# First attention of a fused attention and expert kernel: split q and k for the last three pairs of heads

## The chip, the cores and the metric

The kernel runs on one core of one Trainium2 chip. The metric is the device time of the program in microseconds (us); lower is better. Before the change the median of three runs is 1208.19 us (1207.63 to 1209.15).

## The reference

Four batches of eight heads, 768 positions and 64 columns a head go through softmax attention with a mask and a bias by distance. The result, as rows of 512, goes through four experts whose outputs are added with weights from `domain_probs`.

```python
scores = scale * np.matmul(q, k.transpose(0, 1, 3, 2))        # (4, 8, 768, 768)
is_global = pos[None, :] < int(n_global)                      # 8
is_local = (rel >= 0) & (rel < int(n_local))                  # 96
scores = scores + bias[None, :, :, :]
scores = np.where(keep, scores, -1000000000.0)
a = np.exp(scores - np.max(scores, axis=-1, keepdims=True))
a = a / (np.sum(a, axis=-1, keepdims=True) + 1e-09)
x = (a @ v) as rows of 3072 x 512
for e in range(4):
    h = np.maximum(x @ w1[e], 0.0)
    out += p[:, e:e + 1] * (h @ w2[e])
```

A row of 128 queries needs only the keys of its own tile of 128, the last 96 of the tile before, and the 8 global keys.

## The kernel before, in words

**Attention.** Heads go in pairs, two times 64 columns on 128 partitions. A pair has six tiles of 128 queries. For each tile and head the scores are one block of 256 keys (128 in a first tile): 32 columns of global keys and 96 of the tile before, then 128 of the tile itself.

`attention` (L480) is a generator; each call of its inner `flow` (L486) is one step of a pipeline over tiles. In the step of tile n, `scores` (L386) does the matmuls of tile n into the PSUM tile `ps`, `softmax` (L407) works on the two tiles before, `turn` (L448) transposes the normalised weights `pb` of tile n-3 through PSUM (`pt`) to `pT`, and after every third tile `weigh` (L460) multiplies `pT` by v (`px`) and copies the result to `x`. In `softmax`, VectorE (DVE) adds scores and bias and takes the row's extreme (`nmax`, the operation that the profile calls CUSTOM_DVE_ANT_0), ScalarE (ACT) does exp with the sum to `zsum`, DVE adds 1e-9 to `zsum` (L434), takes the reciprocal (L431) and multiplies `pb` by it (L442).

**Two ways of preparing q and k.** The first batch is computed before any expert work (`early`), the three others are woven into the expert stage.

- Early, `prepare_early` (L358): TensorE (PE) transposes three tiles of q or k of a pair into `pt`. For q, ACT writes the first head's half (L366) and DVE the second's (L370; ACT for the first half of the first pair, L368) into a tile `early_q`, whose other partitions are zeros from `po.memset` (L552, L553, two such tiles); for k, ACT copies both heads at once (L375) and GpSimd (POOL) repeats the global keys (L377). Scores are one full f32 matmul a head (L394).
- Later batches, `prepare_q` (L327) and `prepare_k` (L340): every value is split into a rounded part (F32R) and the rest. For q, ACT writes the rounded part to `st_q` (L331), DVE the rest (L332), and four DMAs on SP's queue place the two heads on the partitions where they are needed, into `qd` (L338). For k, ACT casts each head's half (L351), DVE writes the rests on the other half of the partitions (L354), and DVE repeats the global keys (L356). Scores are two F32R matmuls a head, always 256 keys wide (L398).

**What sets the order.** While `Ordered.on` is true every instruction keeps its program order on its engine; this holds for the whole first attention and the start of the expert stage. Pairs go in the order 0, 2, 1, 3. `prepare_all` (L526) is a generator that prepares one half of q or k at each `next`, and `AHEAD` (L211) says after which tiles the next half comes. In before the order of halves is q, k, k, q for pairs 2 to 4 of that order. In each engine's queue a half stands behind its step's softmax, turn and weigh: on DVE ahead of the next tile's addition of the bias, on ACT behind the two exps, the copy of `pT` and, where there is one, the copy of `x`. SP's queue holds all loads of q, k, v (`start`, L507), the DMAs of shifted v windows (`vg`, L382) and the loads of weights (`raw`, L677, L712), in program order. Chores (L825 to L832) put the splitting of the first experts' weights and of `x` between the steps of the last two pairs.

**Pools** (L824): `st` has one buffer, `qd` one, `kd` two, and there are four `pt` and three `ps` buffers in PSUM.

Of the kernel before, what the change touches and what calls it, by code (L numbers as in the profile page):

```python
# [185 lines left out]
def attn_moe_kernel(ctx: ExitStack, tc, q, k, v, n_global, n_local, domain_probs, w1, w2, out):  # L186
# [88 lines left out]
    class Pools:  # L275


        def __init__(self, stack, name, st, kd, qd, nat, natv, pb, ps, pt, px, early):
            self.early = early

            def sbuf(part, bufs):
                return stack.enter_context(tc.tile_pool(name=f"{name}_{part}", bufs=bufs))

            def psum(part, bufs):
                return stack.enter_context(tc.tile_pool(name=f"{name}_{part}", bufs=bufs, space=PSUM))

            self.st, self.natv = sbuf("st", st), sbuf("natv", natv)
            self.kd, self.qd, self.nat, self.vg = sbuf("kd", kd), sbuf("qd", qd), sbuf("nat", nat), sbuf("vg", kd)
            self.pb, self.pT, self.small = sbuf("pb", pb), sbuf("pT", 4), sbuf("small", pb)
            self.ps, self.pt = psum("ps", ps), psum("pt", pt)  # L290

            self.px, self.pxname = (psum("px", px), "px") if px else (self.pt, "pt")
# [47 lines left out]
    def prepare_k(A, nat, hf, got):  # L340


        tp = transpose_half(A, nat, hf)
        tpv = tp[:, :HALF].rearrange("p (t c) -> p t c", c=P)
        if hf == 0:
            got["k"] = A.kd.tile([P, 2, NQT, PL], F32R, name="kd")
        kd = got["k"]
        pl = slice(hf * TPH, (hf + 1) * TPH)
        for j in range(2):
            own = slice(j * D, (j + 1) * D)  # L350
            ac.copy(kd[own, j, pl, :P], tpv[own])  # L351
        for j in range(2):
            own, oth = slice(j * D, (j + 1) * D), slice((1 - j) * D, (2 - j) * D)
            ve.tensor_tensor(kd[oth, j, pl, :P], tpv[own], f32(kd[own, j, pl, :P]), op=ALU.subtract)  # L354
        if hf == 0:
            ve.tensor_copy(kd[:, :, :, P:], f32(kd[:, :, 0:1, :NGLOB]).to_broadcast([P, 2, NQT, NGLOB]))  # L356

    def prepare_early(A, nat, hf, name, got, zq, first=False):  # L358


        tp = transpose_half(A, nat, hf)
        tpv = tp[:, :HALF].rearrange("p (t c) -> p t c", c=P)
        pl = slice(hf * TPH, (hf + 1) * TPH)
        if name == "q":
            got["q"] = zq
            ac.activation(zq[:D, 0, pl, :], tpv[:D], AF.Copy, scale=-SCALE)  # L366
            if first:
                ac.activation(zq[D:, 1, pl, :], tpv[D:], AF.Copy, scale=-SCALE)  # L368
            else:
                ve.tensor_scalar_mul(zq[D:, 1, pl, :], tpv[D:], -SCALE)  # L370
            return
        if hf == 0:
            got["k"] = A.kd.tile([P, NQT, PL], F32, name="early_k")
        dst = got["k"]
        ac.copy(dst[:, pl, :P], tpv)  # L375
        if hf == 0:
            po.tensor_copy(dst[:, :, P:], dst[:, 0:1, :NGLOB].to_broadcast([P, NQT, NGLOB]))  # L377
# [5 lines left out]
        po.tensor_copy(vg[NPREV:], vt[:NGLOB, :, 0:1, :].to_broadcast([NGLOB, 2, NQT, D]))  # L383
        return vg

    def scores(A, t, got, early):  # L386

        ps = A.ps.tile([P, 2, 2 * P], F32, name="ps")
        c0 = max(t - 1, 0) * PL + (0 if t == 0 else NGLOB)
        n = P if t == 0 else 2 * P  # L390
        for j in range(2):
            if early:
                win = got["k"].rearrange("p t c -> p (t c)")[:, c0 : c0 + n]
                te.matmul(ps[:, j, :n], got["q"][:, j, t, :], win, start=True, stop=True)  # L394
                continue
            win = got["k"][:, j].rearrange("p t c -> p (t c)")[:, c0 : c0 + 2 * P]
            for part in range(2):
                te.matmul(  # L398
                    ps[:, j, : 2 * P],
                    got[("q", t // TPH)][:, j, part, t % TPH * P : (t % TPH + 1) * P],  # L400
                    win,
                    start=(part == 0),
                    stop=(part == 1),
                )
        return ps

    def softmax(A, new, old):  # L407


        if old:  # L410
            pb, zsum = old["pb"], old["zsum"]
        if new:
            t, pr, ps = new["t"], new["pr"], new["ps"]
            cols = slice(0, P) if t == 0 else slice(0, 2 * P)
            bcol = slice(2 * P, 3 * P) if t == 0 else slice(0, 2 * P)
            new["pcol"] = pcol = slice(P, 2 * P) if t == 0 else slice(0, 2 * P)
            nmax = A.small.tile([P, 2], F32, name="nmax")
            new["zsum"] = A.small.tile([P, 2], F32, name="zsum")
            new["pb"] = A.pb.tile([P, 2, 2 * P], F32, name="pb")
        for j in range(2):  # L420
            if new:
                e = new["pb"][:, j, pcol]
                ve.tensor_tensor_reduce(
                    e, ps[:, j, cols], nbias[:, 2 * pr + j, bcol], 1.0, 3.0e38, ALU.add, ALU.min, nmax[:, j : j + 1]
                )
                ac.activation(
                    e, e, AF.Exp, bias=nmax[:, j : j + 1], scale=-1.0, accum_out=new["zsum"][:, j : j + 1]
                )
            if old:
                if j == 1:  # L430
                    ve.reciprocal(zsum, zsum)  # L431
                elif A.early:
                    old["spare"] = A.small.tile([P, 2], F32, name="spare")
                    ve.tensor_scalar_add(zsum, zsum, 1e-9)  # L434
                else:
                    ac.activation(zsum, zsum, AF.Copy, bias=1e-9)
        if old:
            for j in range(2):
                p = pb[:, j, old["pcol"]]
                if A.early:  # L440

                    ve.tensor_scalar(  # L442
                        p, p, zsum[:, j : j + 1], None, op0=ALU.mult, op1=ALU.add, accum_out=old["spare"][:, j : j + 1]
                    )
                else:
                    ac.activation(p, p, AF.Copy, scale=zsum[:, j : j + 1])
# [33 lines left out]
    def attention(b, A, early=False):  # L480
# [5 lines left out]
        def flow(new=None):  # L486

            one, two, three, four = tiles
            if new:
                new["ps"] = scores(A, new["t"], gots[new["pr"]], early)  # L490
            if four:
                turned.append(four)
            ready = len(turned) == TPH
            if ready and not early:
                weigh(A, turned, x)
            if three and not early:
                turn(A, three)
            softmax(A, one, two)
            if three and early:
                turn(A, three)  # L500
            if ready and early:
                weigh(A, turned, x)
            if ready:
                turned.clear()
            tiles[:] = [new, one, two, three]
# [20 lines left out]
        def prepare_all(pr):  # L526

            nat, got = nats[pr], gots[pr]
            got["v"] = nat
            prepare_early(A, nat["q"], 0, "q", got, zqs[PAIRS.index(pr) % 2], first=pr == 0)  # L530
            if pr:
                yield 1
            prepare_early(A, nat["k"], 0, "k", got, zqs[PAIRS.index(pr) % 2])
            yield 1
            nat["vg"] = windows(A, nat["v"])
            prepare_early(A, nat["k"], 1, "k", got, zqs[PAIRS.index(pr) % 2])
            yield 1
            prepare_early(A, nat["q"], 1, "q", got, zqs[PAIRS.index(pr) % 2])
            yield 1

        nats, gots = {}, [{} for _ in range(NPAIR)]
        if early:
# [4 lines left out]
            for h in halves:  # L547
                next(h)
            nats[0]["v"] = next(load(A, v, b, 0, "v"))
            zqs = [A.qd.tile([P, 2, NQT, P], F32, name=f"early_q{n}") for n in range(2)]  # L550
            for zq in zqs:
                po.memset(zq[D:, 0], 0.0)  # L552
                po.memset(zq[:D, 1], 0.0)  # L553
            todo = [prepare_all(pr) for pr in PAIRS]
            next(bias)
            next(todo[0])
# [264 lines left out]
    bp = main.enter_context(tc.tile_pool(name="bp", bufs=1))  # L821
    Ordered.on = True
    with ExitStack() as start_stack:
        A = Pools(start_stack, "start", st=1, kd=2, qd=1, nat=2, natv=3, pb=4, ps=3, pt=4, px=1, early=True)  # L824
        for n, _ in enumerate(attention(0, A, early=True)):  # L825
            if n == 9:
                chores += [load_w1(0, lead=2), load_w2(0, lead=3)]
            if n == 18:
                chores.append(load_w1(1, lead=2, hold=3))
            if n == 2 * NQT + 5:  # L830
                chores.append(blocks(0, (0,), po))
            work_chores()  # L832
        mix = mixture()
        next(mix)
# [85 lines left out]
```

## Time and profile before

| what | value |
|---|---|
| median of three runs | 1208.19 us |
| time of the profiled execution | 1207.05 us |
| its span | 1205.2 us |
| PE busy | 1173.4 us (97%) |
| DVE busy | 830.0 us (69%) |
| ACT busy | 494.8 us (41%) |
| POOL busy | 213.8 us (18%) |
| first attention | from 0 to about 72 us of the span |

The profile is one execution. Its times count from the start of the span; the profiled execution's own time is 1.85 us longer than the span. A row of the time line has the start, the duration, the engine, the line, the operation, what it writes and reads, the shape and, in brackets, how long the engine sat idle before it and what ended this. Nearly every instruction carries L42, the line of the helper that records them, so rows are told apart by the names of tiles. A duration is not the distance to the next start: engines overlap an operation's end with the next one's beginning, so distances between starts are used where a rate matters.

### The profile page before, as it was taken

The page shows a single profiled execution, that of the slowest core. Times are in us where ns is not written, and L with a number is a line of the kernel's source. Part 1 is how long each engine was busy: PE and PEld are TensorE (multiplying, and loading weights), DVE is VectorE, ACT ScalarE, POOL GpSimd, SP SyncE. Part 2 cuts the span into 40 slices and gives each one's busy share as a digit, 9 for nine tenths or more (in the row PEclk, how much of TensorE's full clock was granted, in tenths as well). Part 3 has the DMA queues.
Part 4 walks back from the last instruction along what each step waited for, and adds up shares of the span by engine and source line. Part 5 has one row for each costly group of instructions (what it writes and reads, how often), then busy time and mean ns, then how long its engine had stood idle before and what let it go on. Part 6 is the DMA issues. An engine that isn't in the chain of part 4 may idle for free.

```text
span 1205.2 us, 18090 instructions
## 1 busy us (share of the span) xinstructions
PE 1173.4 (97%) x6624; PEld 1050.4 (87%) x6624; DVE 830.0 (69%) x1841; ACT 494.8 (41%) x1269; POOL 213.8 (18%) x226
## 2 busy tenths in 40 slices
PE   6888999999999999999999999999999999999997
PEld 5677889899889989899898989899898999999996
DVE  6886566666678676676668767576676766666665
ACT  5865656555542444444442444444443211111110
POOL 5546645646450000000002000000000100000000
PEclk9999999999999999999999999999999999999999
DMA  6456786876977656575746757675663655555532
GB/s 164 122 187 213 247 309 224 305 263 243 339 244 251 217 197 210 201 234 171 230 174 201 257 184 221 204 222 169 212 212 133 244 193 193 185 178 183 188 131 90
DMA packets 122704, 251.39 MB, mean 209 GB/s; under 512 B 83184, under 2 KB 91376, under 8 KB 106224
## 3 DMA queue, kind: packets, MB, share of 16 engines
q1 hardware_dynamic: 118864, 243.87, 60.9%
q10 hardware_dynamic: 3744, 6.30, 1.4%
q8 instruction: 54, 0.88, 0.3%
q14 instruction: 42, 0.34, 0.1%
HBM read 174.11 MB, written 52.43 MB: 188 GB/s over the span
## 4 chain that ended last, share of the span: by engine, by line
PE 87%; DVE 3%; DMA 3%; ACT 3%; POOL 2%; issue 2%; SPq 0%; ACTq 0%; POOLq 0%; DVEq 0%
PE pm L42 77%; PE pt L42 6%; PE ps L42 3%; DMA raw<-in_moe_w_dram 2%; DVE pb L42 1%; POOL sums L42 1%; ACT pb L42 1%; POOL w2s L42 1%; DMA qd<-st_q 1%; SPq L42 0%; DVE x L42 0%; DVE zsum L42 0%; DMA raw_ng<-in_n_global_dram 0%; ACT pT L42 0%; ACT w1s L42 0%
## 5 line engine op out<-in xcount | busy, mean ns | idle before, releaser
L42 PE MATMUL pm<-w2s,h 128*128 128x512 f32 x2304 | 551.8, 393 | 4.5 <-DVE h L42 4.5
L42 PEld LDWEIGHTS pm<-w2s,h 128*128 128x128 f32 x2304 | 426.0, 188 | 92.8 <-DVE h L42 6.9
L42 DVE SCALAR_TENSOR_TENSOR acc<-pm,prob,acc 128x512 f32<-128x512 f32 x360 | 268.1, 748 | 148.5 <-PE pm L42 146.3
L42 PE MATMUL pm<-xT,w1s 128*128 128x384 f32 x1536 | 296.5, 338 | 0.2 <-ACT xT L42 0.2
L42 PEld LDWEIGHTS pm<-xT,w1s 128*128 128x128 f32 x1536 | 267.7, 189 | 2.3 <-issue 1.4
L42 PE MATMUL pm<-xB,w1s 128*128 128x384 f32 x1152 | 226.7, 338 | 1.6 <-DVE xB L42 1.3
L42 PEld LDWEIGHTS pm<-xB,w1s 128*128 128x128 f32 x1152 | 201.2, 188 | 6.8 <-DVE xB L42 1.6
L42 ACT ACTIVATE h<-pm 128x384 fp32r<-128x384 f32 x256 | 124.7, 491 | 178.3 <-DVE pm L42 174.8
L42 DVE SCALAR_TENSOR_TENSOR h<-pm,h 128x384 fp32r<-128x384 f32 x256 | 140.7, 552 | 13.6 <-ACT h L42 10.0
L42 ACT ACTIVATE pb<-pb,nmax 128x256 f32<-128x256 f32 (+1 forms) x192 | 93.1, 486 | 102.1 <-DVE nmax L42 97.9
L42 ACT COPY p<-pm 128x384 f32<-128x384 f32 x64 | 30.6, 479 | 190.6 <-PE pm L42 181.7
L42 POOL COPY vg<-v 32x768 f32<-32x768 f32 x16 | 13.2, 823 | 497.6 <-DMA v<-in_v_dram 378.9
L42 DVE TENSOR_TENSOR u<-pm,p 128x384 f32<-128x384 f32 x64 | 35.6, 556 | 73.9 <-PE pm L42 54.3
L42 DVE CUSTOM_DVE_ANT_0 pb<-ps,nbias 128x256 f32<-128x256 f32 (+1 forms) x192 | 71.4, 395 | 8.4 <-PE pt L42 4.7
L42 ACT COPY pT<-pt 128x512 f32<-128x512 f32 (+1 forms) x96 | 52.4, 546 | 56.3 <-PE pt L42 56.0
L42 DVE TENSOR_TENSOR pm<-pm,vv 128x384 f32<-128x384 f32 x128 | 71.6, 560 | 1.6 <-PE pm L42 1.4
L42 ACT ACTIVATE pb<-pb,zsum 128x256 f32<-128x256 f32 (+1 forms) x144 | 63.2, 484 | 18.1 <-DVE zsum L42 18.1
L42 PE MATMUL pt<-ident,pb 128*128 128x128 f32 x352 | 57.5, 277 | 9.1 <-DVE pb L42 5.1
L42 PEld LDWEIGHTS pt<-ident,pb 128*128 128x128 f32 x352 | 42.7, 141 | 19.3 <-ACT pb L42 10.0
L42 DVE TENSOR_TENSOR vv<-pm,u 128x384 f32<-128x384 f32 x64 | 35.7, 557 | 27.7 <-PE pm L42 27.1
L42 DVE TENSOR_TENSOR u<-pm,u 128x384 f32<-128x384 f32 x64 | 35.6, 557 | 25.0 <-PE pm L42 24.3
L42 POOL TENSOR_TENSOR w2s<-raw,w2s 128x512 fp32r<-128x512 f32 x32 | 41.1, 1301 | 57.4 <-ACT w2s L42 50.6
(89 smaller groups left out, 904.4 us busy)
## 6 DMA issues: line engine op xcount, KB each, us to landing
w1s<-kept SPq DMA_DIRECT2D x48, 1792.0 KB, 7.3
w2s<-kept SPq DMA_DIRECT2D x48, 1024.0 KB, 4.9
kept<-w1s SPq DMA_DIRECT2D x16, 1792.0 KB, 9.4
qd<-st_q SPq DMA_DIRECT2D x96, 192.0 KB, 4.7
raw<-in_moe_w_dram SPq DMA_DIRECT2D x32, 512.0 KB, 5.8
kept<-w2s SPq DMA_DIRECT2D x16, 1024.0 KB, 7.1
v<-in_v_dram SPq DMA_DIRECT2D x16, 384.0 KB, 4.0
out_dram<-acc ACTq DMA_DIRECT2D x24, 256.0 KB, 3.3
```

Source lines behind the costliest of these rows:

```text
L42: ins = fn(*args, **kwargs)
```

## The change

In the first attention only the first pair keeps the early form. The three others use `prepare_q` and `prepare_k` with their split parts, DMAs and doubled F32R matmuls; their halves come in the order q, k, q, k, and the shifted windows of v come ahead of the last of them. The early pair's q is now one tile by head, written by ACT in both halves, and only one such tile has its zeros set. The repeat of the global keys in `prepare_k` goes to POOL in the early attention. The addition of 1e-9 writes a third, unused column of `spare` as a sum. `qd` has three buffers.

```diff
-    def prepare_early(A, nat, hf, name, got, zq, first=False):
+    def prepare_early(A, nat, hf, name, got, zq):
...
-            ac.activation(zq[:D, 0, pl, :], tpv[:D], AF.Copy, scale=-SCALE)
-            if first:
-                ac.activation(zq[D:, 1, pl, :], tpv[D:], AF.Copy, scale=-SCALE)
-            else:
-                ve.tensor_scalar_mul(zq[D:, 1, pl, :], tpv[D:], -SCALE)
+            ac.activation(zq[0][:D, pl, :], tpv[:D], AF.Copy, scale=-SCALE)
+            ac.activation(zq[1][D:, pl, :], tpv[D:], AF.Copy, scale=-SCALE)
...
-            ve.tensor_copy(kd[:, :, :, P:], f32(kd[:, :, 0:1, :NGLOB]).to_broadcast([P, 2, NQT, NGLOB]))
+            eng = po if A.early else ve
+            eng.tensor_copy(kd[:, :, :, P:], f32(kd[:, :, 0:1, :NGLOB]).to_broadcast([P, 2, NQT, NGLOB]))
...
-            if early:
+            if early and pr == 0:
...
-                    old["spare"] = A.small.tile([P, 2], F32, name="spare")
-                    ve.tensor_scalar_add(zsum, zsum, 1e-9)
+                    old["spare"] = spare = A.small.tile([P, 3], F32, name="spare")
+                    ve.tensor_scalar(zsum, zsum, 1e-9, None, op0=ALU.add, op1=ALU.add, accum_out=spare[:, 2:3])
...
             if pr:
+                prepare_q(A, nat["q"], 0, got)
                 yield 1
+                prepare_k(A, nat["k"], 0, got)
+                yield 1
+                prepare_q(A, nat["q"], 1, got)
+                yield 1
+                nat["vg"] = windows(A, nat["v"])
+                prepare_k(A, nat["k"], 1, got)
+                yield 1
+                return
...
-            zqs = [A.qd.tile([P, 2, NQT, P], F32, name=f"early_q{n}") for n in range(2)]
-            for zq in zqs:
-                po.memset(zq[D:, 0], 0.0)
-                po.memset(zq[:D, 1], 0.0)
+            zq = f32(A.qd.tile([P, 2, 2, HALF], F32R, name="qd")).rearrange("p j n (t c) -> p j (n t) c", c=P)
+            zq = [zq[:, j] for j in range(2)]
+            po.memset(zq[0][D:], 0.0)
+            po.memset(zq[1][:D], 0.0)
```

How this moves instructions is best seen on DVE in the fifth and sixth tile of the first pair. Before, behind the scaling of `pb` (`pb,spare<-pb,zsum`) the next tile's addition of the bias (`ISA pb,nmax<-ps,nbias`) follows at once, since both steps prepare halves of k on ACT alone:

```order
L42 TENSOR_SCALAR early_q_165<-pt 64x384
L42 ISA pb,nmax<-ps,nbias 128x256
L42 ISA nmax 128x1
L42 TENSOR_SCALAR zsum<-zsum 128x2
L42 ISA pb,nmax<-ps,nbias 128x256
L42 ISA nmax 128x1
L42 RECIPROCAL zsum<-zsum 128x2
L42 TENSOR_SCALAR pb,spare<-pb,zsum 128x256 x2
L42 ISA pb,nmax<-ps,nbias 128x256
```

In the changed kernel two subtractions into `kd` stand at that place:

```order
L42 SCALAR_TENSOR_TENSOR st_q<-pt,st_q 128x384
L42 ISA pb,nmax<-ps,nbias 128x256
L42 ISA nmax 128x1
L42 TENSOR_SCALAR zsum,spare<-zsum 128x2
L42 ISA pb,nmax<-ps,nbias 128x256
L42 ISA nmax 128x1
L42 RECIPROCAL zsum<-zsum 128x2
L42 TENSOR_SCALAR pb,spare<-pb,zsum 128x256 x2
L42 TENSOR_TENSOR kd<-pt,kd 64x3x128 x2
L42 ISA pb,nmax<-ps,nbias 128x256
```

The half of q has kept its place, with another operation; the half of k, which had none on DVE, now has two instructions ahead of the next tile.

The second place is SP's queue from the load of the second next pair's v on. Before:

```order
L42 DMA v<-in_v_dram 128x12x64
L42 DMA vg<-v 96x768
L42 DMA q<-in_q_dram 128x6x64 x2
L42 DMA k<-in_k_dram 128x6x64 x2
L890 TENSOR_LOAD flag
L890 ISA x2
L42 DMA v<-in_v_dram 128x12x64
```

In the changed kernel:

```order
L42 DMA v<-in_v_dram 128x12x64
L42 DMA qd<-st_q 64x768 x4
L899 TENSOR_LOAD flag
L899 ISA x2
L42 DMA qd<-st_q 64x768 x4
L42 DMA vg<-v 96x768
L42 DMA qd<-st_q 64x768 x4
L42 DMA q<-in_q_dram 128x6x64 x2
L42 DMA k<-in_k_dram 128x6x64 x2
L42 DMA v<-in_v_dram 128x12x64
L42 DMA qd<-st_q 64x768 x4
```

Three halves of q, four DMAs each, now stand ahead of the last pair's loads of q and k, and a fourth half comes behind its load of v.

More of the change, by code (lines that the diff above doesn't have):

```diff
@@ L287, in __init__ @@
             self.st, self.natv = sbuf("st", st), sbuf("natv", natv)
+            self.one = sbuf("one", 1) if early else None
             self.kd, self.qd, self.nat, self.vg = sbuf("kd", kd), sbuf("qd", qd), sbuf("nat", nat), sbuf("vg", kd)
@@ L365, in prepare_early @@
             got["q"] = zq
-            ac.activation(zq[:D, 0, pl, :], tpv[:D], AF.Copy, scale=-SCALE)
-            if first:
-                ac.activation(zq[D:, 1, pl, :], tpv[D:], AF.Copy, scale=-SCALE)
-            else:
-                ve.tensor_scalar_mul(zq[D:, 1, pl, :], tpv[D:], -SCALE)
+            ac.activation(zq[0][:D, pl, :], tpv[:D], AF.Copy, scale=-SCALE)
+            ac.activation(zq[1][D:, pl, :], tpv[D:], AF.Copy, scale=-SCALE)
             return
         if hf == 0:
-            got["k"] = A.kd.tile([P, NQT, PL], F32, name="early_k")
+            got["k"] = A.one.tile([P, NQT, PL], F32, name="early_k")
         dst = got["k"]
@@ L384, in windows, with scores @@
         return vg
-    def scores(A, t, got, early):
+    def scores(A, t, pr, got, early):
         ps = A.ps.tile([P, 2, 2 * P], F32, name="ps")
@@ L391, in scores @@
         for j in range(2):
-            if early:
+            if early and pr == 0:
                 win = got["k"].rearrange("p t c -> p (t c)")[:, c0 : c0 + n]
-                te.matmul(ps[:, j, :n], got["q"][:, j, t, :], win, start=True, stop=True)
+                te.matmul(ps[:, j, :n], got["q"][j][:, t, :], win, start=True, stop=True)
                 continue
@@ L489, in flow @@
             if new:
-                new["ps"] = scores(A, new["t"], gots[new["pr"]], early)
+                new["ps"] = scores(A, new["t"], new["pr"], gots[new["pr"]], early)
             if four:
@@ L529, in prepare_all @@
             got["v"] = nat
-            prepare_early(A, nat["q"], 0, "q", got, zqs[PAIRS.index(pr) % 2], first=pr == 0)
             if pr:
+                prepare_q(A, nat["q"], 0, got)
                 yield 1
-            prepare_early(A, nat["k"], 0, "k", got, zqs[PAIRS.index(pr) % 2])
+                prepare_k(A, nat["k"], 0, got)
[6 more added lines that the diff above has]
+                return
+            prepare_early(A, nat["q"], 0, "q", got, zq)
+            prepare_early(A, nat["k"], 0, "k", got, zq)
             yield 1
             nat["vg"] = windows(A, nat["v"])
-            prepare_early(A, nat["k"], 1, "k", got, zqs[PAIRS.index(pr) % 2])
+            prepare_early(A, nat["k"], 1, "k", got, zq)
             yield 1
-            prepare_early(A, nat["q"], 1, "q", got, zqs[PAIRS.index(pr) % 2])
+            prepare_early(A, nat["q"], 1, "q", got, zq)
             yield 1
@@ L823, in attn_moe_kernel @@
     with ExitStack() as start_stack:
-        A = Pools(start_stack, "start", st=1, kd=2, qd=1, nat=2, natv=3, pb=4, ps=3, pt=4, px=1, early=True)
+        A = Pools(start_stack, "start", st=1, kd=2, qd=3, nat=2, natv=3, pb=4, ps=3, pt=4, px=1, early=True)
         for n, _ in enumerate(attention(0, A, early=True)):
```

## The prediction

> **What bounds the kernel now.** The page's chain of what ended last gives 87% of the span to TensorE, but almost all of that is the expert stage. The change touches only the first attention, so I read the stage table for it, then the chain of its first 78 us, then the time line of VectorE (DVE) and ScalarE (ACT) one step at a time.
>
> First the stage table (columns: stretch in us, its length, busy time of PE, PEld, DVE, ACT, POOL, then granted clock, DMA share, GB/s). The first row runs from the step of the third tile to the step behind the last preparation, the second from there to the first expert matmul. Behind it stands the chain by line of 0 to 78 us.
>
> ```profile
> 15.91:48.85 32.94, 29.48 (x232) 23.63 (x232) 26.94 (x137) 27.21 (x86) 15.39 (x19) 1.00 0.52 143
> 48.85:72.28 23.43, 19.05 (x154) 14.26 (x152) 20.20 (x100) 20.94 (x62) 15.81 (x17) 0.93 0.26 56
> by line: DVE pb L42 17.7%; ACT pb L42 10.1%; DMA raw<-in_moe_w_dram 8.8%; PE ps L42 4.8%; DVE zsum L42 4.6%; DMA raw_ng<-in_n_global_dram 4.6%; issue 4.5%; ACT pT L42 4.5%; DVE x L42 4.2%; PE px L42 3.8%; DVE early_q L42 3.6%; PE pt L42 3.4
> DVE early_q L42 <- ACT early_q L42: 7.3, 7, 1.9
> PE pt L42 <- DVE pb L42: 5.1, 8, 1.2
> ```
>
> PE, DVE and ACT are all 82 to 89% busy, so busy shares decide nothing. The chain does: it goes through softmax work of DVE and ACT, and the score matmuls (ps) carry 4.8%. The waits (who waited for whom: total us, times, longest) say the same: PE waits for the softmax of the tile before, and DVE waits 7.3 us for ACT's half of q.
>
> A step is one `flow` call. I count it from the first scores-plus-bias operation (CUSTOM, pb<-ps) of one tile to that of the next. DVE's time line, in pieces:
>
> ```profile
> 18.72 0.42 DVE L42 CUSTOM_DVE_ANT_0 pb<-ps,nbias 128x256 f32<-128x256 f32 x1
> 20.48 0.42 DVE L42 CUSTOM_DVE_ANT_0 pb<-ps,nbias 128x256 f32<-128x256 f32 x1
> ...
> 25.86 0.29 DVE L42 CUSTOM_DVE_ANT_0 pb<-ps,nbias 128x128 f32<-128x128 f32 x1
> 27.36 0.08 DVE L42 DVE_READ_ACCUMULATOR pb<-pb,zsum 128x1 f32 x1
> 28.02 0.56 DVE L42 TENSOR_SCALAR early_q<-pt 64x384 f32<-64x384 f32 x1 [0.58 <-ACT early_q L42]
> 28.59 0.42 DVE L42 CUSTOM_DVE_ANT_0 pb<-ps,nbias 128x256 f32<-128x256 f32 x1
> ...
> 48.85 0.42 DVE L42 CUSTOM_DVE_ANT_0 pb<-ps,nbias 128x256 f32<-128x256 f32 x1
> ```
>
> A step in which half a k is prepared (18.72 to 20.48) takes 1.76 us, DVE's own work, because DVE has nothing to do for k. A step with half a q (25.86 to 28.59) takes 2.73 us with a narrow first tile: DVE's half of q stands in its queue ahead of the next CUSTOM and waits for ACT, which does it behind exp and the copy of pT. So the q step is a loop DVE, ACT, DVE. Its links on ACT:
>
> ```profile
> 29.12 0.51 ACT L42 ACTIVATE pb<-pb,nmax 128x256 f32<-128x256 f32 x1 [1.13 <-DVE zsum L42]
> 30.12 0.56 ACT L42 COPY pT<-pt 128x512 f32<-128x512 f32 x1
> 30.58 0.48 ACT L42 COPY early_k<-pt 128x384 f32<-128x384 f32 x1
> 27.50 0.48 ACT L42 ACTIVATE early_q<-pt 64x384 f32<-64x384 f32 x1
> 24.38 0.48 ACT L42 COPY x<-px 128x384 f32<-128x384 f32 x1
> 24.75 0.48 ACT L42 ACTIVATE early_q<-pt 64x384 f32<-64x384 f32 x1
> ```
>
> CUSTOM to exp 0.50 (28.59 to 29.12 is 0.53, elsewhere 0.47), both exps 1.00 (29.12 to 30.12), pT 0.46, ACT's q to DVE's q 0.52 (27.50 to 28.02), DVE's q 0.57: 3.05 us. With a 128-wide tile CUSTOM and exps are 0.32 shorter, which gives the 2.73 that was measured. A copy of x in the step adds 0.37 (24.38 to 24.75). A pT of a first tile is half as large: I take 0.21 off.
>
> **The change part by part.** *Halves of q, pairs 2 to 4.* ACT writes st_q, DVE's SCALAR_TENSOR_TENSOR reads it. Same place in both queues, same loop; DVE's duration is the same (0.56 before; 0.56 in the last row below). The step stays at 3.05.
>
> *Halves of k.* One ACT copy becomes two casts, and two subtractions appear on DVE ahead of the next CUSTOM. Later batches run this code; there ACT and DVE show
>
> ```profile
> 104.46 0.96 ACT L42 CAST kd<-pt 64x384 fp32r<-64x384 f32 x2
> 105.46 1.12 DVE L42 TENSOR_TENSOR kd<-pt,kd 64x384 fp32r<-64x384 f32 x2 [1.98 <-ACT kd L42]
> 106.61 0.56 DVE L42 SCALAR_TENSOR_TENSOR st_q<-pt,st_q 128x384 fp32r<-128x384 f32 x1
> ```
>
> The first subtraction starts 1.00 us after the first cast, behind both, and the next DVE operation comes 1.15 later. So the k step, free of any ACT link before, becomes the same loop: 0.50 + 1.00 + 0.46 + 1.00 + 1.15 = 4.11 us. Behind the waiting subtraction stand the next CUSTOM, ACT's exp of that tile, and through these PE's transposes.
>
> Step by step from 18.72, with x copies (+0.37), narrow tiles (-0.32) and half pT (-0.21) at their places: k 4.11, q 3.05, k 4.48, q 2.73, k 4.11, q 3.21, k 4.11, none 1.76, q 3.42, k 3.79, q 3.05, k 4.27: 42.1 us. Before, these twelve steps take 48.85 - 18.72 = 30.1 us. Term: **+12.0**. The weights' casts on ACT in the last of these steps lengthened them before; now ACT has 1.15 us and more free in each k step, which hides them.
>
> *Faster scores.* PE's rows, early form (full f32) and split form, each with what comes next on PE, and from the chain a group of P times V:
>
> ```profile
> 17.02 1.03 PE L42 MATMUL ps<-early_k,early_q 128*128 128x256 f32 x4
> 17.88 0.60 PE L42 MATMUL pt<-ident,pb 128*128 128x128 f32 x4
> 18.32 0.49 PE L42 MATMUL pt<-ident,k 128*128 128x128 f32 x3
> 135.02 0.64 PE L42 MATMUL ps<-kd,qd 128*128 128x256 f32 x4
> 135.50 0.60 PE L42 MATMUL pt<-ident,pb 128*128 128x128 f32 x4
> 30.56 1.49 PE px L42 x24
> ```
>
> A tile's scores go from 0.86 to 0.48 us, 0.38 x 15 = 5.7 us of PE time (the three first tiles were 128 wide and gain nothing). PE already waits for DVE and ACT, so I cost it at nothing; -5.7 is the other bound.
>
> A lighter PE could lose its clock. Granted clock by stretch:
>
> ```profile
> 48.00:52.00 4.00, 2.17 (x15) 1.56 (x13) 3.68 (x15) 2.87 (x9) 1.54 (x2) 1.00 1.00 301
> 52.00:56.00 4.00, 3.54 (x27) 2.90 (x27) 3.52 (x18) 3.83 (x13) 2.83 (x3) 0.60 0.75 115
> ```
>
> After a stretch with 2.17 of 4 us busy the clock was 0.60. [...] The trace shows a drop where all idle time of the stretch is 1.83 us, so I keep it as a rival.
>
> *Start.* Two of four memsets go, and DVE's half of pair 1's second q goes to ACT.
>
> ```profile
> 5.42 3.19 POOL L42 MEMSET early_q<- 64x768 f32 x4
> 9.70 2.08 PE L42 MATMUL ps<-early_k,early_q 128*128 128x256 f32 x4 [0.69 <-POOL early_k L42]
> 15.32 0.56 DVE L42 TENSOR_SCALAR early_q<-pt 64x384 f32<-64x384 f32 x1 [1.92 <-ACT early_q L42]
> ```
>
> The memsets hold up POOL's copy of the global keys, for which PE waits 0.69; PE then works without a gap to the q transposes. Term: **-0.7**; bounds 0 and -1.4 (two memsets of 0.8, nearly all of them).
>
> *Sum on the addition.*
>
> ```profile
> L42 DVE TENSOR_SCALAR zsum<-zsum x24: 156/166/1141, 12.2 to 68.8; 128x2 f32<-128x2 f32 x24
> L42 DVE TENSOR_SCALAR_CACHE_REDUCE pb<-pb,zsum x48: 342/475/480, 12.8 to 69.8; 128x256 f32<-128x256 f32 x40, 128x128 f32<-128x128 f32 x8
> 48.83 1.26 POOL L42 TENSOR_TENSOR w1s<-sums,w1s 128x512 fp32r<-128x512 f32 x1 [0.55 <-ACT w1s L42]
> 49.20 0.92 DVE L42 TENSOR_SCALAR zsum<-zsum 128x2 f32<-128x2 f32 x1
> 68.83 0.33 DVE L42 TENSOR_SCALAR zsum<-zsum 128x2 f32<-128x2 f32 x1
> ```
>
> The addition (min/median/max ns) is stretched up to 1141, ending with POOL's operation (48.83 + 1.26 and 49.20 + 0.92 agree); the form with a sum never goes over 480. After 48.85, where DVE is busy 20.20 of 23.43 us, five additions are stretched (the first and the last are shown), by 1.7 us in all over the median. The new form brings an accumulator read like the one of 0.08 at 27.36 above; I estimate 0.07 more in each of 12 steps, 0.8. Term: **-0.9**; bounds -1.7 and +0.8. In the loops before 48.85 it hides in DVE's wait.
>
> *q by way of DMA.* Each half goes through four DMAs on SP, and st_q has one buffer. Rows of all hops, then of those between 90 and 330 us:
>
> ```profile
> L42 SPq DMA_DIRECT2D qd<-st_q x96: 462/592/1722, 98.7 to 883.6; - x96
> DMA to landing us min/median/max: 2.5/4.7/9.7
> DMA to landing us min/median/max: 2.5/3.5/8.3
> ```
>
> The last of four issues 1.8 us after the first and lands 3.5 to 4.7 later, 5.3 to 6.5 in all. ACT wants to write st_q again 5.75 to 6.2 us later (a k step and 1.96): 0.3 to 0.75 late at 4.7, in each of four such gaps, nothing at 3.5. Term **+0.8**, bounds 0 and 1.9. The scores need the hop two steps later and more (over 7 us). SP's loads of the last pair are queued behind three hops now, with some steps to spare. POOL's wider copy of the global keys has POOL's idle time.
>
> Sum: +12.0 - 0.7 - 0.9 + 0.8 = **+11.2**. All later work is ordered behind this stage, so it shifts. The profiled execution took 1207.05 us: 1218.3. The median of the runs shown is 1208.19, 1.1 more; I put the forecast between, at **1218.8**.
>
> **The rivals.** *Work without the loop:* the subtractions cost only their 1.15 each, because their wait falls into waits that are there anyway: 6 x 1.15 = 6.9, less 0.7 and 0.9: +5.3, on the same base 1212.9. For it: q steps could pass on slack. Against it: 24.38 to 24.75 shows ACT without a gap ahead of q.
>
> *PE is the bound (faster):* the scores' 5.7 us come off, with 0.7 and 0.9: -7.3, 1200.3. It decides if PE's gaps before transposes are not real waits for softmax. For it: 29.48 of 32.94 us busy. Against it: PE's wait of 5.1 us for DVE, and 4.8% of the chain.
>
> *Cold PE:* at half clock the four steps with P times V and a preparation become PE's. Scores 0.48, transposes of P 0.44 (17.88 to 18.32), P times V 1.49 (1.24 where a first tile leaves 20 matmuls), three more transposes 0.33: 10.5 us for the four, doubled 20.9, against 15.4 as steps above: +5.5, 1224.3. For it: the clock row. Against it: PE can work ahead of the softmax by most of a step.
>
> *Late hop:* landings of 9.7 instead of 4.7 add 5.0 in each of four gaps: +20, 1238.8. For it: hops share the queue with loads. Against it: both medians. It decides above a landing of about 5 us.
>
> *Absorbed:* the expert stage's start waits for weights anyway and gives the delay back: no change, 1207.6. For it: 8.8% of the chain is such a load. Against it: SP loads these weights behind this stage's work.
>
> **How the numbers follow.** Loop as forecast 0.60 (own range 1216 to 1221), work without the loop 0.12, cold PE 0.09, late hop 0.07, PE the bound 0.06, absorbed 0.06. A range of 1212 to 1224.5 holds the first three, 0.81. A measurement of this kernel can tell about 0.2% (2.4 us) from no change. Faster 0.06, same 0.06, slower 0.88.
>
> **What would show it.** Right: kd subtractions on DVE with an idle time of about 1 us ahead "<-ACT kd", k steps near 4 us, scores of four matmuls in 0.48 us with longer PE gaps, no zsum over 300 ns, the first expert matmul near 83 us. Wrong: k steps near 3 us, PE without gaps, or st_q waiting for qd by several us.

## The result, and the profile after

The changed kernel takes 1221.08 us in the median of four runs (1219.72 to 1221.65), beside 1208.67 us (1207.63 to 1210.01) for the kernel before: a ratio of 1.0101 [1.0089, 1.0113], 12.4 us slower. The profiled execution took 1221.65 us, its span is 1219.9 us and its mean granted clock 0.988 (before 0.996). Medians and ratios are of executions in the fast state; one slow execution of the experiment with the sum alone (1300.35 us at a granted clock of 0.85) is left out.

The difference arises in the first attention: 13.0 of the 14.7 us between the two profiled spans stand before the first expert matmul. The other 1.7 are within the scatter of the stretch behind it, which takes 1131.9 to 1134.6 us in the profiles of all kernels here. A step is named by pair and tile in order of work (1.5 is the sixth tile of the second pair) and lasts from its first CUSTOM on DVE to the next tile's.

| us | before | after | difference | forecast |
|---|---|---|---|---|
| step 0.3 starts | 18.72 | 16.97 | -1.75 | -0.7 |
| twelve steps, 0.3 to 2.2 | 30.13 | 45.71 | +15.58 | +12.8 (loop and hop) |
| from 2.3 to the first expert matmul | 23.43 | 22.60 | -0.83 | -0.9 |
| first expert matmul | 72.28 | 85.28 | +13.0 | +11.2 |

The stage table with the same columns as in the prediction, first the twelve steps before, then the two stretches of the changed kernel:

```profile
18.72:48.85 30.13, 26.67 (x214) 21.10 (x214) 24.56 (x126) 25.48 (x80) 15.39 (x19) 1.00 0.47 134
16.97:62.68 45.71, 31.11 (x219) 25.66 (x217) 29.61 (x150) 30.33 (x86) 16.19 (x19) 0.81 0.72 191
62.68:85.28 22.60, 16.82 (x150) 13.16 (x150) 19.24 (x110) 20.63 (x62) 15.26 (x16) 0.92 0.32 65
```

PE, DVE and ACT were 82 to 89% busy in these steps and are now 65 to 68% busy: each is idle for about a third of the time. The granted clock fell from 1.00 to 0.81.

DVE's time line of the changed kernel:

```profile
16.50 0.56 DVE L42 SCALAR_TENSOR_TENSOR st_q<-pt,st_q 128x384 fp32r<-128x384 f32 x1 [1.56 <-ACT st_q L42]
16.97 0.41 DVE L42 CUSTOM_DVE_ANT_0 pb<-ps,nbias 128x256 f32<-128x256 f32 x1
...
19.89 1.12 DVE L42 TENSOR_TENSOR kd<-pt,kd 64x384 fp32r<-64x384 f32 x2 [1.07 <-ACT kd L42]
21.04 0.42 DVE L42 CUSTOM_DVE_ANT_0 pb<-ps,nbias 128x256 f32<-128x256 f32 x1
...
28.76 1.12 DVE L42 TENSOR_TENSOR kd<-pt,kd 64x384 fp32r<-64x384 f32 x2 [2.32 <-ACT kd L42]
...
46.29 0.42 DVE L42 CUSTOM_DVE_ANT_0 pb<-ps,nbias 128x256 f32<-128x256 f32 x1
...
51.10 0.56 DVE L42 SCALAR_TENSOR_TENSOR st_q<-pt,st_q 128x384 fp32r<-128x384 f32 x1 [2.97 <-ACT st_q L42]
51.57 0.28 DVE L42 CUSTOM_DVE_ANT_0 pb<-ps,nbias 128x128 f32<-128x128 f32 x1
...
62.68 0.42 DVE L42 CUSTOM_DVE_ANT_0 pb<-ps,nbias 128x256 f32<-128x256 f32 x1
```

The first two CUSTOM rows show the forecast loop: from 16.97 to 21.04 is 4.07 us where 1.76 stood before, and the subtractions between them come after 1.07 us idle behind ACT's casts. The row at 28.76 is that of step 0.5, where the wait is 2.32. The rows from 46.29 to 51.57 show what was not forecast: the q step 1.5 takes 5.28 us, with DVE idle for 2.97 until ACT's half of q. Step by step:

| step | 0.3 k | 0.4 q | 0.5 k | 1.0 q | 1.1 k | 1.2 q | 1.3 k | 1.4 | 1.5 q | 2.0 k | 2.1 q | 2.2 k |
|---|---|---|---|---|---|---|---|---|---|---|---|---|
| forecast | 4.11 | 3.05 | 4.48 | 2.73 | 4.11 | 3.21 | 4.11 | 1.76 | 3.42 | 3.79 | 3.05 | 4.27 |
| measured | 4.07 | 3.56 | 5.31 | 2.73 | 4.06 | 3.77 | 4.05 | 1.77 | 5.28 | 3.73 | 3.13 | 4.25 |

Eight steps agree within 0.08 us. Steps 0.4, 0.5, 1.2 and 1.5 are 0.51, 0.83, 0.56 and 1.86 too long, 3.8 in all. Around step 1.5, the windows of the changed kernel, PE's time line and two of PE's rows of before for comparison:

```profile
40.00:44.00 4.00, 1.32 (x8) 0.95 (x8) 2.88 (x14) 2.41 (x7) 0.00 (x0) 0.99 1.03 254
43.50:44.00 0.50, 0.00 (x0) 0.00 (x0) 0.49 (x2) 0.00 (x0) 0.00 (x0) 0.94 0.90 227
44.00:44.50 0.50, 0.00 (x0) 0.00 (x0) 0.50 (x1) 0.00 (x0) 0.00 (x0) 0.50 0.90 326
44.00:48.00 4.00, 1.88 (x12) 1.43 (x14) 3.92 (x22) 2.87 (x10) 0.00 (x0) 0.50 0.93 235
48.00:52.00 4.00, 4.00 (x33) 3.67 (x30) 1.03 (x8) 2.04 (x5) 2.87 (x5) 0.65 0.56 187
```

```profile
42.05 0.85 PE L42 MATMUL pt<-ident,pb 128*128 128x128 f32 x4 [2.10 <-ACT pb L42]
46.12 1.21 PE L42 MATMUL pt<-ident,pb 128*128 128x128 f32 x4 [2.73 <-DVE pb L42]
47.26 0.69 PE L42 MATMUL px<-pT,v 128*64 128x128 f32 x4
47.74 0.64 PE L42 MATMUL px<-pT,vg 128*64 128x128 f32 x4
48.17 0.64 PE L42 MATMUL px<-pT,v 128*64 128x128 f32 x4
```

```profile
38.17 0.39 PE L42 MATMUL px<-pT,vg 128*64 128x128 f32 x4
38.39 0.39 PE L42 MATMUL px<-pT,v 128*64 128x128 f32 x4
```

After a stretch with 1.32 of 4 us busy the granted clock falls from 1.00 to 0.50 at about 43.9, and the work that starts at 46.12 runs at about half speed: four matmuls of P times V take 0.43 us from start to start (47.74 to 48.17; before 0.22, from 38.17 to 38.39), and PE is busy without a gap from 48 to 52. ACT's copy of x and then its half of q wait for this, 1.33 and 0.39 us.

The hop shows in PE's time line for the first scores of the second pair, and in the summary of the addition's tile the sum:

```profile
22.35 0.47 PE L42 MATMUL ps<-kd,qd 128*128 128x256 f32 x2 [2.61 <-DMA qd<-st_q]
23.50 0.77 PE L42 MATMUL ps<-kd,qd 128*128 128x256 f32 x2 [0.67 <-DMA qd<-st_q]
```

```profile
L42 DVE TENSOR_SCALAR_CACHE_REDUCE zsum<-zsum x24: 143/150/155, 11.3 to 82.0; 128x2 f32<-128x2 f32 x24
```

PE wants the first hop 2.61 us before it has landed. No addition is stretched any more: the longest of 24 took 155 ns.

### The profile page after: what moved, and what is told of

It is laid out like the page before. It is cut to its first block, busy times and chain, and to the rows that moved or that the text cites. A ratio compares the mean times of both kernels' runs of the same rounds, so it can differ in the third digit from the quotient of the medians.

```text
span 1219.9 us, 18190 instructions
## 1 busy us (share of the span) xinstructions
PE 1176.6 (96%) x6624; PEld 1054.7 (86%) x6624; DVE 833.1 (68%) x1876; ACT 500.3 (41%) x1276; POOL 213.0 (17%) x224
## 4 chain that ended last, share of the span: by engine, by line
PE 84%; DMA 5%; ACT 3%; DVE 3%; issue 2%; POOL 2%; SPq 1%; ACTq 0%; POOLq 0%; DVEq 0%
PE pm L42 75%; PE pt L42 6%; PE ps L42 3%; DMA qd<-st_q 3%; DMA raw<-in_moe_w_dram 2%; DVE pb L42 1%; ACT pb L42 1%; POOL sums L42 1%; SPq L42 1%; POOL w2s L42 1%; PE px L42 0%; DVE kd L42 0%; ACT kd L42 0%; DVE x L42 0%; DMA q<-in_q_dram 0%
## 5 line engine op out<-in xcount | busy, mean ns | idle before, releaser
L42 PE MATMUL ps<-kd,qd 128*128 128x256 f32 x360 | 61.6, 291 | 4.7 <-DMA qd<-st_q 4.7
L42 PEld LDWEIGHTS ps<-kd,qd 128*128 128x128 f32 x360 | 55.4, 194 | 9.1 <-POOL kd L42 2.8
```

The costliest lines, as they stand in the source:

```text
L42: ins = fn(*args, **kwargs)
```

## The experiments

The theory: the k halves' wait on DVE for ACT closes a loop, and that loop is the loss. The rivals: the added work by itself; PE (scores, cold clock); the hop by way of DMA. Ratios are to the kernel before, with 95% intervals; "end" is the first expert matmul in the profile (before 72.28, after 85.28). An end comes from one profile of each kernel, and up to 1.1 us of a difference between two ends can be the start of the program alone (the section behind this one has the figures).

**The loop in the kernel before.** The k halves of the last three pairs are copied by head on ACT and two subtractions that nobody reads follow on DVE. Scores, memsets and addition are as before, and there is no hop.

```diff
-        ac.copy(dst[:, pl, :P], tpv)
...
+            for j in range(2):
...
+                ac.copy(dst[own, pl, :P], tpv[own])
+            for j in range(2):
...
+                ve.tensor_tensor(rest[oth], tpv[own], dst[own, pl, :P], op=ALU.subtract)
```

> The kernel before, scores and q untouched, where each half of k of the last three pairs is copied to its tile in two halves by ACT and two subtractions on DVE, of the size and the place of the changed kernel's, read it and write a tile that nobody uses. It adds work and leaves nothing out. Loop theory (DVE, waiting for ACT's copies, holds up the next tile's softmax): the k steps go from 1.5 to 2.5 us to about 4.1, the whole costs about as much as the change, 1220.5 us (1218.5 to 1222), 12 over before. Work alone: 6 x 1.15 = 6.9 more, 1215.5. If the change's cost lies in the DMA hop of q or in a cold PE: within 3 us of before, 1209 to 1212.

Measured: 1.0131 [1.0116, 1.0147], 1222.87 us, end 87.70. DVE's time line, and the windows around step 1.5:

```profile
17.94 0.42 DVE L42 CUSTOM_DVE_ANT_0 pb<-ps,nbias 128x256 f32<-128x256 f32 x1
20.86 1.12 DVE L42 TENSOR_TENSOR rest<-pt,early_k 64x384 fp32r<-64x384 f32 x2 [1.07 <-ACT early_k L42]
22.00 0.42 DVE L42 CUSTOM_DVE_ANT_0 pb<-ps,nbias 128x256 f32<-128x256 f32 x1
```

```profile
44.00:48.00 4.00, 2.03 (x12) 1.27 (x13) 3.91 (x20) 2.70 (x10) 2.47 (x4) 0.50 0.02 7
48.00:52.00 4.00, 4.00 (x31) 3.52 (x28) 1.05 (x4) 2.00 (x5) 0.24 (x1) 0.67 0.00 0
```

The same step of 4.06 us with the same wait of 1.07: the wait and its work alone cost as much as the whole change and the two gains that are missing here, which puts the time a little above the expected range. Step 1.5 takes 5.34 us with the same clock of 0.50, while the DMA share is 0.02 and 0.00: at that place the DMA has no part in it.

**The subtractions one step later.** In the changed kernel the two subtractions and the repeat of the global keys are issued at the end of the next softmax, when ACT's casts are long done.

```diff
+        if A.early:
+            held.append(rests)
...
+        while A.early and held:
+            held.pop(0)()
```

> The changed kernel with each pair of k subtractions (and the repeat of the global keys behind them) put one step later on DVE, behind the next tile's softmax, where ACT's casts are long done. Same work, no wait. Loop theory: a k step and the q step behind it fall from about 7.2 us to about 5.5, given back in part because q's DMAs then have less time: 1214 us (1211 to 1217). Work alone: the same work is done, 1221 as the changed kernel. Hop theory: slower or the same, 1221 to 1223.

Measured: 1.0072 [1.0059, 1.0086], 1216.45 us, end 81.80. The wait for kd, in the waits of the changed kernel and then of this one from 10 to 88 us, is nearly gone:

```profile
DVE kd L42 <- ACT kd L42: 8.1, 6, 2.3
```

```profile
DVE kd L42 <- ACT kd L42: 1.4, 1, 1.4
```

Yet only 3.5 of 13.0 us come back. ACT's time line shows one of the waits that took its place; in step 2.1 (7.88 us) ACT's queue stands behind a cast whose weights are not there:

```profile
49.72 0.62 ACT L42 CAST w2s<-raw 128x512 fp32r<-128x512 f32 x1 [3.49 <-DMA raw<-in_moe_w_dram]
```

And step 0.4 takes 6.45 us, in which PE's scores wait for the later repeat of the global keys and then for the hop:

```profile
21.65 0.77 PE L42 MATMUL ps<-kd,qd 128*128 128x256 f32 x2 [2.72 <-POOL kd L42]
23.27 0.77 PE L42 MATMUL ps<-kd,qd 128*128 128x256 f32 x2 [0.85 <-DMA qd<-st_q]
```

**Without the hop.** In the changed kernel the scores read st_q (three buffers) and the four DMAs go; the kernel leaves out the placing of the two heads.

```diff
+        if A.early:
+            got[("q", hf)] = st.rearrange("p (o n) c -> p o n c", o=1)
+            return
...
```

> The changed kernel without q's DMAs in the first attention: the scores of the last three pairs read the split q where ACT and DVE wrote it (three buffers of it), so the placing of the two heads is left out; the matmuls keep number and size. Loop theory with the hop as a small term: PE's 3.3 us and ACT's 0.7 us of waiting for q's DMAs go, worth 1.5 to 3 us, 1219 us (1217.5 to 1220). If the hop were the main cost: 1213 or less.

Measured: 1.0090 [1.0074, 1.0105], 1218.9 us, end 83.71. The twelve steps take 44.51 us, 1.2 less: steps 0.4, 0.5 and 1.2 fall from 3.56, 5.31 and 3.77 to 3.14, 4.80 and 3.30, so the hop had most of what was too long in 0.4 and 1.2 and more than half in 0.5. Step 1.5 stays at 5.24, with a clock of 0.50.

**Both: later subtractions and no hop.**

```diff
+            got[("q", hf)] = st.rearrange("p (o n) c -> p o n c", o=1)
...
+            held.append(rests)
...
```

> The changed kernel with the k subtractions one step later and without q's DMAs in the first attention (the placing of the two heads is left out, as in the kernel without the hop). Loop theory with a DMA queue that took back the gain: with neither, a k step and the q step behind it take about 5.3 us instead of 7.2 and no step waits for q's DMAs or for the weights; against 1.009 without the hop alone, 5 to 7 us less, a ratio to before of 1.004 (1.002 to 1.0055). If DVE's work alone, not its wait, is the cost: 1.008 to 1.009.

Measured: 1.0033 [1.0021, 1.0045], 1210.93 us, end 75.75. DVE's time line of the first k half:

```profile
17.91 0.42 DVE L42 CUSTOM_DVE_ANT_0 pb<-ps,nbias 128x256 f32<-128x256 f32 x1
19.77 1.12 DVE L42 TENSOR_TENSOR kd<-pt,kd 64x384 fp32r<-64x384 f32 x2
21.18 0.56 DVE L42 SCALAR_TENSOR_TENSOR st_q<-pt,st_q 128x384 fp32r<-128x384 f32 x1 [0.28 <-ACT st_q L42]
```

The subtractions start at once, and the half of q behind them waits only 0.28: one step's wait covers the other's work. The four kernels together (ends, in us over before):

| | kd's wait as in the change | subtractions later |
|---|---|---|
| with hop | +13.0 | +9.5 |
| without hop | +11.4 | +3.5 |

The wait is worth 3.5 with the hop and 7.9 without it; the hop 1.6 with the wait and 6.0 without. Either one hides behind the other, so neither of the single experiments shows what it is worth. The twelve steps alone, which leave the start out, say the same: 45.71 us and 41.70 in the upper row, 44.51 and 35.59 in the lower, so the wait is worth 4.0 with the hop and 8.9 without. So do the medians: 12.4, 8.9, 11.3 and 3.3 us over before. The work that stays costs 3.5, net of the start and the addition; in the twelve steps it is 5.5.

**Weights asked for earlier.** As the second experiment, with the loads of the first expert's weights one step earlier.

```diff
-            if n == 9:
-                chores += [load_w1(0, lead=2), load_w2(0, lead=3)]
+            if n == 8:
+                chores += [load_w1(0, lead=3), load_w2(0, lead=4)]
```

> The changed kernel with the k subtractions one step later, as before, and the first loads of expert weights issued one step earlier (ahead of one hop of q) and used at the same step. In the kernel without it one step took 7.9 us, with ACT waiting 3.5 us for these weights. If the weights are what took back the gain of the loop: 3 us less, a ratio to before of 1.0045 (1.003 to 1.0055). If something else fills that step: no change, 1.007.

Measured: 1.0080 [1.0066, 1.0095], end 85.05: neither of the two expected ratios. The wait for weights goes, and ACT's time line shows what comes instead:

```profile
51.62 0.49 ACT L42 ACTIVATE st_q<-pt 128x384 fp32r<-128x384 f32 x1 [5.77 <-DMA qd<-st_q]
```

The hop, now queued behind the weights, holds up st_q's only buffer for 5.77 us. With the hop first on the queue (second experiment) ACT waited 3.49 us for the weights, with the weights first 5.77 us for the hop.

**Scores twice.** In the changed kernel each split score matmul is issued twice: more PE time, and a busier PE.

```diff
-            for part in range(2):
+            for part in (0, 1, 0, 1) if early else (0, 1):
```

> The changed kernel with the split score matmuls of the last three pairs issued twice (the second time starts the sum anew), which takes PE's time for them from 0.48 to about 0.95 us a tile. Loop theory: PE is not the bound, 1221 us within 1.5. Cold clock theory: a busier PE keeps its clock, the steps with P times V get 2 to 3 us shorter in all, 1218.5. PE as the bound: 18 x 0.48 = 8.6 us more, 1229.

Measured: 1.0120 [1.0104, 1.0135], 1221.78 us, end 85.46: the interval overlaps the change's, so doubling these matmuls costs nothing that can be told. Seven of the twelve steps (0.3, 1.0, 1.1, 1.3, 1.4, 2.1, 2.2) keep their time within 0.04 us. The windows, and ACT in step 2.0:

```profile
44.00:48.00 4.00, 2.11 (x25) 1.61 (x26) 3.81 (x23) 3.10 (x10) 0.00 (x0) 1.00 0.91 238
48.00:52.00 4.00, 4.00 (x34) 3.83 (x35) 2.02 (x12) 1.40 (x4) 1.44 (x3) 1.00 0.81 248
```

```profile
51.60 0.62 ACT L42 CAST w2s<-raw 128x512 fp32r<-128x512 f32 x1 [2.57 <-DMA raw<-in_moe_w_dram]
```

The clock stays at 1.00 and step 1.5 falls from 5.28 to 3.49 us, near the forecast 3.42. But the cast of weights that follows cannot start before 51.60 (after: 51.05), and step 2.0 grows from 3.73 to 5.98. The same with the loads one step earlier:

```diff
+            for part in (0, 1, 0, 1) if early else (0, 1):
...
+                chores += [load_w1(0, lead=3), load_w2(0, lead=4)]
```

> The changed kernel with the split scores issued twice, as before, and the first loads of expert weights one step earlier. Issued twice alone, one step with P times V fell from 5.3 to 3.5 us and the next, waiting for weights, grew from 3.7 to 6.0. Cold clock theory: with the weights in time the 1.8 us stay, a ratio to before of 1.0085 (1.007 to 1.0095) where the changed kernel has 1.0101. If the clock costs nothing: 1.010 to 1.011.

Measured: 1.0104 [1.0088, 1.0119], end 85.95. Step 1.5 takes 6.05 us. Now the hop ends last there, on ACT's time line:

```profile
51.28 0.49 ACT L42 ACTIVATE st_q<-pt 128x384 fp32r<-128x384 f32 x1 [2.60 <-DMA qd<-st_q]
```

PE at a clock of 0.50 (the changed kernel), weights (scores twice) and hop (here) let ACT go on at 50.58, 51.60 and 51.28. And without any hop:

```diff
+            got[("q", hf)] = st.rearrange("p (o n) c -> p o n c", o=1)
...
+            for part in (0, 1, 0, 1) if early else (0, 1):
...
```

> The changed kernel without q's DMAs and with the split scores issued twice (the placing of the heads is left out). Without the hop the weights come in time, so a gain by a warmer PE is not taken back: cold clock theory, the step with P times V that takes 5.2 us falls to 3.5, 2 us in all, a ratio to before of 1.0072 (1.006 to 1.0085). If the clock costs nothing: as without the hop, 1.009.

Measured: 1.0099 [1.0083, 1.0114], 1219.09 us, end 83.58, within the interval of the kernel with single scores. It tells less than was meant, since the clock fell here all the same:

```profile
44.00:48.00 4.00, 3.16 (x24) 2.68 (x24) 2.79 (x18) 3.01 (x10) 1.01 (x2) 0.57 0.02 5
```

Step 1.5 takes 4.73 us against 5.24. The variants of the changed kernel with a clock of 1.00 at that place have a DMA share of 0.91 to 1.04 from 44 to 48 us, and none of the three with doubled scores is faster than the kernel with single scores (1.0101, without the hop 1.0090). So what the clock costs in the total stays open, and may be nothing; in the step itself it is up to 1.8 us (5.28 against 3.49). A low clock by itself does not make the step long: in the kernel with both edits (later subtractions, no hop) PE's groups of P times V are 0.43 us apart there too, but they begin 0.3 us ahead of the step, and the step takes 3.70.

**The sum alone**, in the kernel before.

```diff
-                    ve.tensor_scalar_add(zsum, zsum, 1e-9)
+                    ve.tensor_scalar(zsum, zsum, 1e-9, None, op0=ALU.add, op1=ALU.add, accum_out=spare[:, 2:3])
```

> The kernel before with one part of the change alone: the addition of 1e-9 on DVE also writes an unused sum. If the form with a sum does not wait for POOL and its read is hidden (the changed kernel's steps of 1.76 us say so): the five stretches behind 48.85 us go, 1.7 us, and part of two earlier ones, 1206 us where before is 1207.6 to 1208.7, a ratio of 0.9975 to 0.9988. If the accumulator read costs the 0.07 us a step that the prediction took: 0.8 less gain, a ratio of 0.999 to 1.

Measured: 0.9983 [0.9974, 0.9991], 1205.97 us beside 1207.94; end 71.40, 0.88 earlier.

**Two memsets later.** In the kernel before, the second pair of memsets comes behind POOL's first copy of the global keys.

```diff
+            zeros(zqs[0])
             todo = [prepare_all(pr) for pr in PAIRS]
...
             next(todo[0])
+            zeros(zqs[1])
```

> The kernel before with the second pair of memsets put behind POOL's first copy of the global keys, DVE still writing its half of q. One look at the start: as the prediction has it, the memsets are all of the start's gain and the first step of the fourth tile begins 0.7 us earlier, at 18.0. If the move of DVE's half of q to ACT is what made 1.75 us: 18.0 to 18.7 here, too, and the rest is that move; if the memsets made it: 17.0.

One profiled execution, 1207.17 us; step 0.3 starts at 17.40, 1.32 earlier, and the end is 71.23, 1.05 earlier. PE's time line of before and of this kernel, then that of the loop experiment, whose instructions up to here are those of before:

```profile
12.21 1.92 PE L42 MATMUL ps<-early_k,early_q 128*128 128x256 f32 x4
13.92 0.85 PE L42 MATMUL pt<-ident,q 128*128 128x128 f32 x3
```

```profile
11.16 1.91 PE L42 MATMUL ps<-early_k,early_q 128*128 128x256 f32 x4
12.87 0.58 PE L42 MATMUL pt<-ident,q 128*128 128x128 f32 x3
```

```profile
12.18 1.48 PE L42 MATMUL ps<-early_k,early_q 128*128 128x256 f32 x4
13.49 0.49 PE L42 MATMUL pt<-ident,q 128*128 128x128 f32 x3
```

The memsets are worth 12.21 - 11.16 = 1.05 us. The other 0.27 are the transposes of q behind it, 0.58 instead of 0.85 us. Such a difference comes without any edit too: in the loop experiment the same two instructions take 1.48 and 0.49 instead of 1.92 and 0.85, and step 0.3 starts at 17.94 instead of 18.72. (The granted clock of before is 1.00 from 8 to 16 us, with the longer durations; what makes them differ was not shown.)

**q on ACT.** In the kernel before, all halves of q go by head to ACT, as the change does for the first pair, with the addition's sum and the later memsets; k and scores as before.

```diff
-                ve.tensor_scalar_mul(zq[D:, 1, pl, :], tpv[D:], -SCALE)
...
+            ac.activation(zq[1][D:, pl, :], tpv[D:], AF.Copy, scale=-SCALE)
```

> The kernel before with the sum on the addition, q in one tile by head for all pairs, both heads' halves of q always written by ACT, and the second pair of memsets put behind the start. So no preparation has anything on DVE, and no step is a loop. Loop theory: q steps go from about 3.05 us to ACT's own 2.3, 2.6 us less over the preparation, with 1.7 from the start and 1.7 from the sum about 6 less than before: a ratio of 0.995 (0.9935 to 0.9965). If ACT's load or PE sets these steps: a ratio of 0.997 to 0.999.

Measured: 0.9950 [0.9937, 0.9963], 1202.58 us beside 1207.94, end 67.97: the best version. Its twelve steps:

```profile
15.43:43.11 27.68, 25.85 (x218) 21.41 (x217) 20.57 (x131) 27.11 (x82) 13.85 (x17) 1.00 0.53 141
```

27.68 us instead of 30.13, with ACT busy for 27.11 of them; step 0.3 starts 3.3 us earlier, and the part behind step 2.3 is 1.4 longer. DVE's wait for ACT's half of q, 5.0 us before in the five q steps (0.5, 1.0, 1.3, 1.5, 2.2), is gone: these take 6.3 us less, the other seven 3.8 more, as ACT now sets them. Of the 4.3 us by which the end comes earlier, the later memsets (1.05) and the sum (0.88) gave 1.9 alone; the other 2.4 come with the move of q, the scatter of the start included.

## Why the prediction was right, and where it was off

**The loop (+12.0): right.** The k steps 0.3, 1.1, 1.3, 2.0 and 2.2, priced at 3.79 to 4.27, came within 0.06 us, with idle times of 0.99 to 1.34 where 1.00 was taken. The loop alone reproduces the loss, and without wait and hop only 3.5 of 13.0 us are left. "Work without the loop" falls as the account of the change, but with both waits nearly gone its size was about right: the twelve steps cost 5.5 us where it had 6.9.

**The hop (+0.8, up to 1.9): right kind, too small, and its reason failed.** Taking it away saves 1.2 us in the twelve steps. The step that failed is "the scores need the hop two steps later and more (over 7 us)": PE runs ahead of the softmax, wanted the first hop at 22.35 - 2.61 = 19.74, 2.7 us after DVE had finished that half (17.06), and waited. Its rival "late hop" named the shared queue, but the sum gave no price to hop and weights standing behind one another, which the earlier loads show (5.77 us); in the change this is covered by the loop.

**Cold PE: counted as a rival, it came beside the loop.** In the changed kernel groups of four matmuls of P times V start 0.44 us apart in the mean in three of the four weigh steps of the twelve and 0.37 in the fourth; before, 0.23. The rival's price for the four steps was 20.9 us against 15.4; they took 18.6. Most of that is step 1.5: 5.28, 5.34 and 5.24 us at a clock of 0.50, with the hop, without any split scores, and without the hop, and 3.49 at 1.00 with the scores twice. In step 2.2 a clock of 0.50 from 58 to 61 us cost nothing (4.25 against 4.27 forecast). What spoke against it, that PE works ahead, holds in 1.2 and 2.2, where P times V begins 2.0 and 1.2 us ahead of the step. In 0.5 it begins 0.5 behind, since the hop held PE back (without the hop 0.4 ahead), and in 1.5 it begins 1.0 behind, since the short step 1.4 leaves PE with softmax results only at 46.12.

The sum has no term for the clock. In the changed kernel the clock fell to 0.50 at about 43.9, when PE had been idle for 0.6 us (its scores end at 43.38); the gap before that is the 2.10 us ahead of 42.05. Low busy shares stand ahead of this drop and of the one in the row of before, which is at 0.50 from 53 to 56 us (1.32 and 2.17 of 4 us), but doubled scores kept a clock of 1.00 behind a stretch with 2.11, so these rows do not show what makes the clock fall.

**Faster scores (0): right.** Issuing them twice changes the time by nothing that can be told. The 0.48 us a tile did not show: from a tile's four score matmuls to PE's next instruction it is 0.55 to 1.00 us in the changed kernel where PE goes on at once.

**Start (-0.7, bounds 0 and -1.4): mis-sized, beyond its bound.** Measured -1.75. The term was read from PE's idle time of 0.69 for POOL; the memsets alone gave 1.05, because PE's next group also follows the one before without a break (one row of eight matmuls, 2.90 us from 7.83). Up to 0.78 more can be the difference between profiles of the same code, as between before and the loop experiment (18.72 and 17.94). The changed kernel and its seven variants, whose compute work up to there is the same, reach step 0.3 at 16.10 to 17.20 us, so the -1.75 from one profile of each kernel carries about a microsecond of such scatter. What q on ACT does for the first pair was not tried alone.

**Sum on the addition (-0.9): right.** The part behind step 2.3 is 0.83 shorter, and the edit alone ends the stage 0.88 earlier. The accumulator's read (76 to 85 ns each), priced at 0.8, hides: step 1.4, which has no preparation, takes 1.77 after and 1.76 before.

**The sum.** The start came out 1.05 better than its term, the twelve steps 2.8 worse than loop and hop, the rest 0.07 worse: 11.2 became 13.0. The errors have opposite signs, so that the time lands only 2.3 us above the forecast is in part luck: the mechanism of the k steps was right, while the twelve steps as a whole were 2.8 too short. "Absorbed", "PE is the bound" and "late hop" fall: the delay is passed on, doubled scores cost nothing, and st_q waits for the hop 0.7 us in all.

## What to carry to other kernels

Where two engines hand work to each other inside a step, price an edit by where its wait stands in the in-order queue: an instruction ahead of the next tile's first operation puts the other engine's whole queue on the path, and moving DVE's half of q away from that place, with the two gains of 1.9 us beside it, made the kernel 0.5% faster although it added work to ACT. When one wait is removed and little comes back, look for the next one before giving up the theory: here wait and hop hid each other, and only the four kernels with and without both showed it. PE's clock can go as well: in the changed kernel it fell from 1.00 to 0.50 behind a stretch with 1.32 of 4 us busy. What makes it fall was not shown. Where a trace shows such a drop and PE cannot work ahead, price its work at the measured rate too (groups of P times V 0.43 us apart here, 0.22 before).

## What the runs showed of the hardware that was not expected

- The granted clock of the changed kernel fell from 1.00 to 0.50 at about 43.9 us, when PE had been idle for 0.6 us, and the gap before that was 2.10 us. With doubled scores and no hop it fell too, to 0.57 in the window from 44 to 48 us, while doubled scores with the hop kept 1.00 there.
- In the kernel before, the addition on 128x2 was stretched up to 1141 ns while POOL worked (42.68 + 1.14 us beside POOL's 42.51 + 1.29); the same with a sum took 143 to 155 ns in all 24 places, and its read of 76 to 85 ns did not show (step 1.4: 1.77 us, before 1.76).
- The start of the program is not the same in each profile: before and the loop experiment run the same instructions up to step 0.3 and reach it at 18.72 and 17.94 us, with PE's transposes of q at 0.85 and 0.49 us; the granted clock of before is 1.00 from 8 to 16 us.
- With four SP DMAs for each half of q and the first weights on one queue, the DMA share of the changed kernel stood at 1.03 and 0.93 from 40 to 48 us (without the hop 0.81 and 0.00). With the hop in place, each experiment that removed another wait met the end of a transfer next (3.49, 2.57, 5.77 and 2.60 us).
